# Fifteen products instead of sixteen, forked partial sums and one timed plan in a fused convolution and SwiGLU kernel

## The chip, the cores and the metric

The kernel runs on one core of one Trainium2 chip. The metric is device time of one execution in microseconds (us), lower is better. A time quoted here is the median of the fast runs of one kernel; all runs of this study were fast ones. A change of more than 2% either way counts as faster or slower, and less counts as the same.

Engines are written as in the profile: PE is TensorE's matmuls, PEld its weight loads, DVE is VectorE, ACT is ScalarE, POOL is GpSimd, SP issues transfers. "L436" is line 436 of the kernel in question. An edit that adds a line moves the numbers behind it: L586 is L587 in some experiments.

## The reference

The input is x of (8, 4096, 192) in float32. A causal convolution with 7 taps comes first (one softmaxed set of taps for each of 8 heads of 24 channels). Its 32768 tokens are normalised and go through a feed-forward block with an inner width of 1536:

```python
out = np.einsum('hk,bskhg->bshg', w, x_unf)           # 7 shifted copies of x, weighted
rms = np.sqrt(np.mean(x * x, axis=-1, keepdims=True) + 1e-06)
xn = x / rms * rms_g
g = xn @ w_gate                                        # 192 -> 1536
silu = g * (1.0 / (1.0 + np.exp(-g)))
val = xn @ w_val                                       # 192 -> 1536
return (silu * val @ w_out).astype(np.float32)         # 1536 -> 192
```

## The kernel before

The kernel works through 32 pairs of blocks of 512 tokens. For each pair there are two phases on TensorE.

In the **gate-and-value phase** four units each multiply a 3 x 3 block of weights with blocks of the normalised activations. A scheme in the manner of fast matrix multiplication needs fewer block products than plain multiplication, and pays for it with sums of weights (made once), sums of activations (`x_sums`, made for every pair on VectorE) and combinations of partial sums. Each product consists of two halves (gate in the lower rows of the array, value in the upper). The first pair uses plain products while the weight sums are made.

In the **output phase** 384 matmuls of 192 columns multiply the activated values with `w_out`. Beside it the other engines prepare later inputs: convolution, norm and transposes (`front`) for the pair after the next, and the sums of activations for the next pair.

```python
def mm(i, bk, x, first=False):                         # one product, both halves (L436)
    for h in range(2):
        rows = HALF[h]
        rhs = x[rows]
        nc.tensor.matmul(
            out=bank(h, bk)[:], lhsT=wf[u][rows, at[i], :], rhs=rhs,
            start=first, stop=True, skip_group_check=True,
        )
# ... 16 calls of mm in a unit, with copies (keep), results (res), silu and mul between them

def evac(dst, bk, n):                                  # a finished output group leaves its bank
    nc.scalar.copy(out=dst, in_=bank(0, bk)[:, 0:n])
    nc.vector.tensor_tensor(out=dst, in0=bank(1, bk)[:, 0:n], in1=dst, op=ALU.add)

# ... convolution: ScalarE multiplies each head's slice, VectorE adds a tap's product
    m = y if k == 0 else prods.tile([P, NJ, D], F32, name="m")
    for h in range(H):
        hs = slice(h * GS, (h + 1) * GS)
        nc.scalar.mul(m[:, :, hs], xk[:, :, hs], taps[:, h, k : k + 1])
    if k > 0:
        nc.vector.tensor_tensor(out=y[:], in0=y[:], in1=m[:], op=ALU.add)

# ... the driver: which step of the side work is emitted beside which group of matmuls
for p in range(PAIRS):
    # ... four units, the transposes of nxt are stepped inside them
    nxt = front(p + 2)
    sums = x_sums(p + 1)
    # ... outer(p, hts, aside): aside steps nxt and, late in the phase, sums
```

## Time and profile before

| what | value |
|---|---|
| time, median of 3 runs | 2837.64 us (2837.35 to 2837.96) |
| span of the profiled run | 2835.1 us |
| gate-and-value phase, 31 times | 54.93 us |
| output phase, 32 times | 31.33 us |
| time before the first output phase | 124.7 us |

The page's first part gives each engine's busy time, its share of the span and its count of instructions:

```profile
PE 2776.3 (98%) x20512; PEld 2206.5 (78%) x20512; DVE 2090.6 (74%) x3178; ACT 1975.9 (70%) x4753; POOL 465.3 (16%) x409
```

Two stretches of the kernel before are one output phase and the gate-and-value phase after it. The columns of this view are the window, the busy time of PE, PEld, DVE, ACT and POOL with instruction counts, the granted TensorE clock (1.00 is full), the DMA share and GB/s (the first window begins 0.27 us into its phase of 31.33 us):

```profile
988.14:1019.20 31.06, 31.06 (x383) 30.90 (x381) 20.42 (x25) 25.62 (x79) 2.06 (x2) 1.00 0.40 109
1019.20:1074.14 54.94, 54.94 (x261) 38.26 (x259) 43.98 (x74) 36.34 (x71) 10.93 (x9) 1.00 0.10 23
```

The reader should see three things: PE is busy for the whole of both windows, the clock is at full speed, and VectorE and ScalarE still have several free microseconds in each. VectorE is idle for 10.6 us of the output phase, so the engine has room for more work there, if that work comes in a good order.

### The profile page before, as it was taken

Reading aid. Unit: us, or ns where it says so; the run is one execution under the profiler, and the core shown is the slowest. Engines: PE = TensorE matmul, PEld = TensorE weight load, DVE = VectorE, ACT = ScalarE, POOL = GpSimd, SP = SyncE. Lnnn points to the kernel's source line nnn. Section 1 sums busy time; section 2 is a strip of 40 time slices with the busy share of each in tenths; the row PEclk is TensorE's granted clock in tenths of the full one; section 3 lists DMA queues with packets and bytes.
Section 4 is the critical chain, followed back from the end, with each engine's and each line's share of the span. In section 5 each row is a group of like instructions: output and inputs, shape, how many; then the busy total and the mean of one; then the engine's idle time right before and its main releaser. Section 6 shows DMA issues by size and latency. Waiting matters only on the chain.

```text
span 2835.1 us, 53033 instructions
## 1 busy us (share of the span) xinstructions
PE 2776.3 (98%) x20512; PEld 2206.5 (78%) x20512; DVE 2090.6 (74%) x3178; ACT 1975.9 (70%) x4753; POOL 465.3 (16%) x409
## 2 busy tenths in 40 slices
PE   3899999999999999999999999999999999999999
PEld 1577888778887788887788877788877888877887
DVE  7677777777777877777777777777777777777754
ACT  6567777667777677776677776777776777766733
POOL 1711111111111111111111111111111111111100
PEclk9999999999999999999999999999999999999999
DMA  6211221212221212221112212112211122111110
GB/s 156 70 48 49 65 65 46 54 43 54 65 64 42 51 46 60 65 56 43 43 54 65 65 40 59 43 54 65 60 40 50 47 65 65 48 51 43 35 45 12
DMA packets 95597, 155.18 MB, mean 55 GB/s; under 512 B 6896, under 2 KB 64752, under 8 KB 91256
## 3 DMA queue, kind: packets, MB, share of 16 engines
q1 hardware_dynamic: 94272, 150.20, 20.6%
q8 instruction: 160, 2.62, 0.4%
q0 software_dynamic: 512, 1.57, 0.2%
q14 instruction: 93, 0.76, 0.1%
q10 hardware_dynamic: 560, 0.03, 0.0%
HBM read 101.44 MB, written 50.33 MB: 54 GB/s over the span
## 4 chain that ended last, share of the span: by engine, by line
PE 97%; DVE 1%; POOL 1%; DMA 0%; issue 0%; ACT 0%; SPq 0%; DVEq 0%; POOLq 0%
PE ps L436 60%; PE ps L559 35%; PE ps L540 1%; POOL wf L228 0%; DVE nt L360 0%; DVE ht L547 0%; DMA xb<-xd 0%; DMA xd<-nt 0%; DVE wf L207 0%; POOL wf L231 0%; ACT y L344 0%; POOL o_sb L141 0%; POOL wo_sb L199 0%; DVE mf_i L202 0%; POOL r L335 0%
## 5 line engine op out<-in xcount | busy, mean ns | idle before, releaser
L436 PE MATMUL ps<-xc,wf 64*128 64x512 f32 x4960 | 1365.2, 589 | 0.0
L436 PEld LDWEIGHTS ps<-xc,wf 64*128 64x128 f32 x4960 | 781.7, 187 | 330.9 <-issue 25.5
L559 PEld LDWEIGHTS ps<-wo_sb,ht 64*128 64x128 f32 x12288 | 1013.3, 187 | 8.9 <-DVE o_sb L568 4.1
L559 PE MATMUL ps<-wo_sb,ht 64*128 64x192 f32 x12288 | 1018.1, 323 | 0.0
L436 PE MATMUL ps<-xb,wf 64*128 64x512 f32 x2976 | 939.5, 589 | 0.0
L444 ACT COPY tp<-ps 128x512 f32<-128x512 f32 x1240 | 659.9, 588 | 300.4 <-PE ps L436 300.4
L456 ACT ACTIVATE sg<-sg 128x512 f32<-128x512 f32 x744 | 475.6, 639 | 289.3 <-DVE sg L453 289.3
L436 PEld LDWEIGHTS ps<-xb,wf 64*128 64x128 f32 x2976 | 488.7, 187 | 190.1 <-issue 13.3
L453 DVE TENSOR_TENSOR sg<-ps,tp 128x512 f32<-128x512 f32 x620 | 422.8, 682 | 212.4 <-ACT tp L444 210.7
L308 DVE TENSOR_TENSOR y<-y,m 128x1536 f32<-128x1536 f32 x190 | 335.0, 1763 | 291.7 <-ACT m L304 291.3
L304 ACT ACTIVATE m<-x_sb,taps 128x192 f32<-128x192 f32 x1520 | 532.7, 441 | 6.8 <-DMA x_sb<-in_x_dram 6.1
L459 DVE TENSOR_TENSOR ht<-ht,sg 128x512 f32<-128x512 f32 x744 | 483.0, 680 | 0.0
L453 DVE TENSOR_TENSOR ht<-ps,tp 128x512 f32<-128x512 f32 x620 | 420.4, 678 | 0.0
L468 POOL TENSOR_TENSOR tp<-tp,sg 128x512 f32<-128x512 f32 x124 | 179.7, 1449 | 1208.9 <-ACT tp L444 1175.2
L332 POOL TENSOR_SCALAR r<-ss 128x8 f32<-128x8 f32 x32 | 10.0, 313 | 1075.8 <-ACT sq L320 1049.0
L568 DVE TENSOR_TENSOR o_sb<-ps,o_sb 128x192 f32<-128x192 f32 (+1 forms) x192 | 75.7, 420 | 116.6 <-ACT o_sb L567 116.6
L468 POOL TENSOR_TENSOR tp<-tp,ht 128x512 f32<-128x512 f32 x124 | 157.8, 1272 | 0.0
L344 ACT ACTIVATE y<-y,r 128x192 f32<-128x192 f32 x252 | 94.0, 445 | 84.5 <-POOL r L335 84.5
L453 DVE TENSOR_TENSOR sg<-tp,ps 128x512 f32<-128x512 f32 x124 | 85.3, 688 | 84.8 <-ACT tp L444 64.3
L567 ACT COPY o_sb<-ps 128x192 f32<-128x192 f32 (+1 forms) x192 | 66.9, 363 | 89.4 <-PE ps L559 89.2
L320 ACT ACTIVATE sq<-y 128x192 f32<-128x192 f32 x252 | 91.7, 364 | 50.6 <-DVE y L308 43.7
L540 PE MATMUL ps<-xb,wf 64*128 64x512 f32 x288 | 71.2, 626 | 54.5 <-DMA xb<-xd 44.4
(52 smaller groups left out, 773.1 us busy)
## 6 DMA issues: line engine op xcount, KB each, us to landing
xb<-xd SPq DMA_DIRECT2D x128, 384.0 KB, 6.3
x_sb<-in_x_dram SPq DMA_DIRECT2D x24, 1344.0 KB, 5.7
xd<-nt SPq DMA_DIRECT2D x128, 192.0 KB, 3.3
out_dram<-o_sb SPq DMA_DIRECT2D x64, 384.0 KB, 2.6
x_sb<-in_x_dram SPq DMA_DIRECT2D x8, 1176.0 KB, 9.1
ht<-in_moe_w_gate_dram SPq DMA_DIRECT2D x12, 192.0 KB, 8.5
ht<-in_moe_w_val_dram SPq DMA_DIRECT2D x12, 192.0 KB, 6.3
o_sb<-in_moe_w_out_dram POOLq DMA_DIRECT2D x8, 192.0 KB, 2.7
```

The source lines that it names most:

```text
L304: nc.scalar.mul(m[:, :, hs], xk[:, :, hs], taps[:, h, k : k + 1])
L308: nc.vector.tensor_tensor(out=y[:], in0=y[:], in1=m[:], op=ALU.add)
L320: nc.scalar.activation(out=sq[:], in_=y[:, j, :], func=AF.Square, accum_out=ss[:, j : j + 1])
L344: nc.scalar.mul(y[:, j, :], y[:, j, :], r[:, j : j + 1])
L436: nc.tensor.matmul(out=bank(h, bk)[:], lhsT=wf[u][rows, at[i], :], rhs=rhs, start=first, stop=True, skip_group_check=True,)
L444: nc.scalar.copy(out=t[:], in_=bank(h, bk)[:])
L453: nc.vector.tensor_tensor(out=dst, in0=in0, in1=in1, op=op)
L456: nc.scalar.activation(out=og[o][:], in_=og[o][:], func=AF.Silu)
L459: nc.vector.tensor_tensor(out=ov[o], in0=ov[o], in1=og[o][:], op=ALU.mult)
L468: nc.gpsimd.tensor_tensor(out=t[:], in0=sb["a", h][:], in1=o3, op=ALU.add)
L540: nc.tensor.matmul(out=bank(h, bk)[:], lhsT=wf[u][HALF[h], k * NF + f, :], rhs=xb[HALF[h], g, k, :], start=(k == 0), stop=(k == KP - 1), s ...
L559: nc.tensor.matmul(out=bank(h, bk)[:, w : w + D], lhsT=hts[f // NF][HALF[h], g, f % NF, j * P : (j + 1) * P], rhs=wo_sb[HALF[h], f, :], st ...
```

## The change

The intent is to take one product in sixteen out of the phase that TensorE bounds. It has five parts:

1. **15 products for 16**, with 11 sums of activations instead of 8.
2. **Forks**: a partial sum that two results need is copied from bank to bank, and both go on accumulating. The output phase writes at most 384 of a bank's 512 columns, and a new "filler" matmul of 128 columns writes the rest. No run leaves the filler out, so what happens without it is not shown.
3. **One timed plan**: a list with a time for each step of a unit, in hundredths of a product; a unit takes 1509 of them. The upper half lags 135 behind the lower one. Everything, the output phase too, goes through one heap ordered by time.
4. **Other engines**: five of six SwiGLU multiplies of a unit move to GpSimd. The first two taps of the convolution are made by VectorE alone.
5. **Transposes in the output phase**: the whole of `front` is now spread over it.

```diff
-    NW = 16
+    NW = 15
+    XOP = (5, 6, 9, 0, 15, 14, 4, 7, 13, 10, 2, 11, 12, 8, 3)
+    XSUM = (
+        (0, 1, 4), (1, 2, 6), (2, 0, 6), (9, 3, 5), (3, 3, 8), (4, 7, 15), (5, 4, 15), (6, 5, 7),
+        (7, 0, 1), (8, 1, 2), (9, 8, 15),
+    )
+    SPAN, PLAN = 1509, (
+        (0, 0, "T", "P", 4, 11, ()), (100, 0, "T", "P", 1, 4, ()), (135, 1, "T", "P", 4, 11, ()),
+        # ... cut: time, half, engine, action, operands, what it frees
+        (1840, 0, "A", "G", 3, ()), (1959, 1, "G", "M", 3, ("g3",)),
+    )
...
+    STEP = 100 * D / T
+    OUT = 2 * (T // P) * FC * STEP
+    OVER = 120
...
+        def evac(dst, bks, w):
+            put(base + n * STEP + OVER, functools.partial(low, dst, bks, w))
+            put(base + n * STEP + LAG + OVER, functools.partial(upp, dst, bks, w))
...
-        nxt = front(p + 2)
-        sums = x_sums(p + 1)
-        # ... cut: the steps beside each group
+        spread(x_sums(p + 1), base + 1650, 160, len(XSUM))
+        spread(front(p + 2, 2), base + 30, 60, 60)
+        emit(base + OUT)
```

The heap fixes the order of each engine's instructions. `spread(it, start, gap, n)` puts n steps of a generator at equal distances. The plan's times are only an order: an instruction that comes late holds up what waits for it (in the trace below PE stands still for 2.07 us, for an eviction that VectorE reaches after an addition of 1.75 us).

## The prediction

> **What bounds the kernel now.** I read the chain of work that ended last first, because a share of busy time does not say which engine sets the end.

> ```profile
> PE 97%; DVE 1%; POOL 1%; DMA 0%; issue 0%; ACT 0%; SPq 0%; DVEq 0%; POOLq 0%
> ```

> That is the page's share of the chain by engine. Its pieces in order of time (start, length, what) are:

> ```profile
> 846.66 54.94 PE ps L436 x256
> 901.60 31.33 PE ps L559 x382
> 932.93 54.94 PE ps L436 x256
> 987.87 31.33 PE ps L559 x382
> 1019.20 54.94 PE ps L436 x256
> ```

> The kernel alternates between a gate-and-value phase (L436, four units of 16 products) and an output phase (L559). PE does both without a gap, in a period of 54.94 + 31.33 = 86.27 us, 31 times. A product (two halves, two passes each) costs 54.94 / 64 = 0.858 us. So a removed product pays in full, if the other engines let PE run on.

> Second, what a step of the other engines costs, and when the chain that prepares later inputs runs. These are ScalarE, then VectorE and GpSimd, from the timeline around the same output phase:

> ```profile
> 989.70 2.86 ACT L304 ACTIVATE y<-x_sb,taps 128x192 f32<-128x192 f32 x8
> 992.47 9.08 ACT L304 ACTIVATE m<-x_sb,taps 128x192 f32<-128x192 f32 x26
> ...
> 1003.57 7.71 ACT L304 ACTIVATE m<-x_sb,taps 128x192 f32<-128x192 f32 x22
> ...
> 1013.10 0.36 ACT L320 ACTIVATE sq<-y 128x192 f32<-128x192 f32 x1 [1.33 <-DVE y L308]
> ...
> 1019.41 0.80 ACT L344 ACTIVATE y<-y,r 128x192 f32<-128x192 f32 x2 [2.44 <-POOL r L335]
> ...
> 1020.47 2.18 ACT L344 ACTIVATE y<-y,r 128x192 f32<-128x192 f32 x6
> ```

> ```profile
> 1011.31 1.76 DVE L308 TENSOR_TENSOR y<-y,m 128x1536 f32<-128x1536 f32 x1 [1.00 <-ACT m L304]
> ...
> 1013.45 1.89 DVE L393 TENSOR_TENSOR xc<-xb 128x512 f32<-128x512 f32 x3
> ...
> 1017.79 0.69 DVE L393 TENSOR_TENSOR xc<-xc 128x512 f32<-128x512 f32 x1
> ```

> The convolution fills ScalarE from 989.4 to 1011.8 (26 steps in 9.08 us: 0.345 us from start to start), then squares (0.49 us each), GpSimd's power (2.3 us), eight scalings that end at 1022.65. That is 34.8 us after the output phase began and 3.4 us after it ended: the transposes come later still, in the gate-and-value phase, where VectorE has room. The eight sums that the next products read end at 1018.48, 0.7 us before they are needed. This order is what the change alters.

> [...]GpSimd's add (L468, first half) took 1.52 us in the 90 cases where it met a VectorE multiply of two SBUF tiles, 1.27 us in the 34 others.
> [...]

> **The change part by part.**

> *Products.* 15 for 16, but the plan gives a unit 1509 hundredths of a product: 4 x 0.91 x 0.858 = 3.12 us less per pair, 31 pairs: -96.9 us (at 15.00 it would be -106).

> *Filler.* One product of 128 columns per output phase: 128/512 x 0.858 = 0.21 us, x 32 = +6.9 us.

> *The units' other engines.* In a unit of 1509 slots (12.95 us) VectorE has 19 steps of about 0.60 us (three sums took 1.89): 11.4 us. ScalarE has 14 copies of about 0.48 and six Silus of 0.53: 9.9 us. GpSimd has 7 steps of 1.27 to 1.45: 8.9 to 10.2 us. None exceeds 12.95. The tightest loop is product at slot 900, fork on ScalarE, product at 1105: 205 slots, 1.76 us. A product's second pass starts 0.43 us after its first, takes 0.59, ScalarE starts 0.04 later, a copy takes 0.59: 1.65 us and a hand-off. It fits, barely.[...] I expect units close to the plan.

> *The output phase.* Here ScalarE loses 16 of 56 convolution steps (-5.5 us); VectorE gains 8 scalings (0.23), 8 multiply-adds (0.33), loses one add of 1.76, and gains 3 sums (0.60) and 6 transposes (0.48). VectorE's total is some 28 of 31.5 us, so the sum fits. The order does not. In the built program VectorE's queue reads: the additions of the convolution, sums 1 to 5, three transposes, a sum, two transposes, a sum, a transpose, four sums. A transpose needs all eight scalings, and the second product of the next unit reads xc[9], which the eleventh sum writes. So PE now waits for the whole convolution chain. From the start of the output phase, at best:
> - two Silus end at 1.4; 40 convolution steps (13.8), one more Silu (0.5), one eviction (0.3): 16.1
> - last addition 1.8: 17.9
> - 8 squares 3.9 and two evictions 0.5: 22.3
> - GpSimd 2.4: 24.7; 8 scalings 2.8: 27.5
> - 6 transposes 2.9, 6 sums 3.6, an eviction 0.5: 34.5

> PE would want that product at 31.33 + 0.21 + 0.86 = 32.4. That is at least 2.1 us of waiting in each of 30 output phases (the last two prepare nothing).

> It may be worse. At the start of the phase three multiplies of the last unit, which the change gives to GpSimd, fall among VectorE's scalings and multiply-adds[...]: up to 3 x 1.27 us of VectorE time. About 1.4 us of delay is free; beyond it the first addition frees a product buffer too late and ScalarE waits at the fourth group. That adds 0 to 2.5 us. I choose 1.5: 3.6 us per phase, x 30 = +108 us. Bank waits inside the phase (the fifth output group needs the bank that an eviction behind the last addition frees, at about 18 to 20 us instead of 16.7) hide under this later wait.

> Sum: 2837.6 - 96.9 + 6.9 + 108 = 2855.6, say 2856 us.

> **The rivals.**
> (a) *PE stays the bound, the gain arrives*: 2837.6 - 96.9 + 6.9 = 2748 us. For it: PE was never made to wait before, and all sums of engine time fit. Against it: the order above, whose durations are those of the same instructions in this trace.
> (b) *The wait is at its floor*, with GpSimd harmless: 2748 + 30 x 2.1 = 2811 us.[...]
> (c) *The units miss the plan too*, through the 1.76 us loop or VectorE at 88%: each hundredth of a product per unit is 1.06 us, so a unit of 15.3 adds 22 us: about 2878 us[...].

> **Range and chances.** The floor of the wait is arithmetic on measured durations, so I give (a) little: it needs an error in my reading of the queue. 2% faster is below 2781 us, a wait under 1.1 us per phase: 0.07. 2% slower is above 2894, a wait of 4.9 us, or 4 with slow units: 0.17. The rest 0.76. The range runs from just below (b) to about (c): 2808 to 2900 us.

> **What would show it.** The chain: a gate-and-value phase of about 51.8 us instead of 54.94, and an output phase with its wait of 34 to 36 us, with sums and transposes on VectorE, scalings on ScalarE and GpSimd's power in the chain where before PE was 97%. Among the waits, PE waiting for a VectorE xc sum about 30 times, 2 to 5 us each. ScalarE's scalings ending about 27.5 to 30 us after the phase begins, and VectorE idle for some us before its first transpose. VectorE's multiply-adds longer than 0.41 us where a GpSimd multiply runs. The prediction is wrong if PE waits under 1 us at the start of the first unit (then my order or chain is wrong), if the units themselves take over 13.2 us each, or if PE loses its time inside the output phase at the banks and not at its end.

## The result

| kernel | median us | range | runs |
|---|---|---|---|
| before | 2837.73 | 2837.35 to 2837.96 | 4 |
| after | 2886.26 | 2885.67 to 2886.68 | 4 |

The ratio is 1.0171 (95% interval 1.0153 to 1.0189): 1.7% slower, which counts as the same. Here and below a ratio is the mean time of one kernel's fast runs over that of the other's of the same rounds, so it is not quite the ratio of the quoted medians.

The prediction of 2856 us and +18 us fell short: the measured difference is +48.5 us. The time is inside the range of 2808 to 2900 us, in part by luck: no term of the prediction had the clock in it, which turns out below to cost some 39 us.

### The profile after

The busy times, and the shares of the last chain by engine, from the page of the changed kernel:

```profile
PE 2761.5 (96%) x20144; PEld 2074.2 (72%) x20144; DVE 2433.6 (84%) x3845; ACT 2088.3 (72%) x4769; POOL 1231.5 (43%) x1033
...
PE 74%; DVE 14%; ACT 7%; issue 4%; POOL 0%; DMA 0%; DVEq 0%; SPq 0%; POOLq 0%
```

PE held 97% of the chain before; now it shares it with VectorE and ScalarE. PE's busy time fell by only 14.8 us although a fifteenth of the products' work is gone (the plan alone should save 96.9 us), so PE is also slower at what is left. The chain in order of time around one output phase (it begins at 1001.63 and ends at 1038.01; columns: start, length, what) shows where it leaves PE:

```profile
1011.77 1.75 DVE y L358
...
1013.55 1.89 ACT m L354 x6
...
1018.01 1.40 ACT m L354 x4
...
1019.62 0.15 DVE y L358
...
1021.29 0.36 DVE o_sb L610
...
1021.70 12.79 PE ps L586 x133
...
1039.46 48.02 PE ps L507 x219
```

The chain passes through the convolution (L354, L358) to an eviction (L610) and only then to PE. It does not pass through the transposes or the eleventh sum, as the prediction had it. The windows of the same phase, with the columns as before:

```profile
1001.63:1019.63 18.00, 17.93 (x205) 17.01 (x201) 17.69 (x27) 16.14 (x46) 4.43 (x4) 1.00 0.41 89
1019.63:1021.70 2.07, 0.01 (x2) 0.01 (x1) 2.07 (x4) 0.29 (x2) 0.00 (x0) 1.00 0.50 119
1022.40:1025.80 3.40, 3.40 (x26) 3.40 (x24) 2.25 (x6) 2.89 (x14) 0.22 (x1) 0.50 0.60 247
1025.80:1038.01 12.21, 12.21 (x155) 12.21 (x153) 7.30 (x14) 3.24 (x9) 2.07 (x2) 1.00 0.27 65
1038.01:1089.88 51.87, 51.87 (x248) 29.73 (x248) 45.65 (x73) 42.29 (x78) 30.75 (x25) 1.00 0.06 16
```

Read the second and third lines. PE stands still for 2.07 us in the middle of the phase, and shortly after that its granted clock is 0.50 for 3.4 us. That stretch holds 26 matmuls (22 of them start in it) where a full clock would give about 43 (the fourth line has 155 in 12.21 us, 12.7 per us). The last line is the gate-and-value phase: 51.87 us at full clock, with PE busy throughout, close to the plan's 4 x 15.09 x 0.858 = 51.8.

Why PE stands still is seen in VectorE's timeline (start, length, engine, line, operation, shapes, count; in brackets the idle time before and what ended it):

```profile
1002.40 2.99 DVE L339 TENSOR_SCALAR y<-x_sb,taps 128x192 f32<-128x192 f32 x8
...
1011.77 7.33 DVE L358 TENSOR_TENSOR y<-y,m 128x1536 f32<-128x1536 f32 x4
1019.02 0.69 DVE L440 TENSOR_TENSOR xc<-xb 128x512 f32<-128x512 f32 x1
1019.62 1.75 DVE L358 TENSOR_TENSOR y<-y,m 128x1536 f32<-128x1536 f32 x1
1021.29 0.35 DVE L610 TENSOR_TENSOR o_sb<-ps,o_sb 128x192 f32<-128x192 f32 x1
...
1030.90 1.58 DVE L410 STREAM_TRANSPOSE nt<-y 128x256 f32<-128x256 f32 x3 [4.73 <-ACT y L394]
...
1037.16 0.67 DVE L440 TENSOR_TENSOR xc<-xc 128x512 f32<-128x512 f32 x1
```

The eviction at 1021.29 frees the bank that the fifth output group needs. The eviction stands in VectorE's queue behind a sum and behind the last addition of the convolution (1019.62 to 1021.37), so PE stops at 1019.63 and goes on at 1021.70. The eleventh sum ends at 1037.83, and PE reaches the product that reads it no earlier than that. The waits of PE over the whole run (total us, times, longest) confirm that this is every phase's pattern:

```profile
PEld ps L586 <- DVE o_sb L610: 70.7, 30, 2.4
...
PE ps L586 <- DVE o_sb L610: 61.8, 30, 2.1
...
PEld ps L586 <- DVE ht L529: 10.8, 29, 0.4
```

The list has no wait of PE for an xc sum at all. A run has 30 such output phases (the last two prepare nothing). In 23 of them the clock dropped to half for 3.41 us after the pause (in one of these for twice as long); in 7 it did not.

### Where the time went

From the spans of the two profiled runs, in us:

| part | before | after | difference |
|---|---|---|---|
| up to the first output phase | 124.7 | 121.7 | -3.0 |
| 31 gate-and-value phases | 1702.9 | 1613.8 | -89.1 |
| 32 output phases | 1007.5 | 1148.7 | +141.2 |
| span | 2835.1 | 2884.2 | +49.1 |

By the medians an output phase with a clock drop takes 36.43 us, one without takes 34.75, and before they took 31.33. The drop therefore costs 1.68 us, half of the 3.41 us. The gate-and-value phase that follows a phase without a drop takes 52.67 instead of 51.87: there PE is early enough to wait 0.8 us for the eleventh sum. (The profile puts this wait down to a ScalarE copy; that it is the sum's is shown by e1, which moves only the sums and takes it away.)

### The profile page after: what moved, and what is told of

Its sections match the earlier page's. It is cut to its first block, busy times and chain, and to the rows that moved or that the text cites. A ratio compares the mean times of both kernels' runs of the same rounds, so it can differ in the third digit from the quotient of the medians.

```text
span 2884.2 us, 53991 instructions
## 1 busy us (share of the span) xinstructions
PE 2761.5 (96%) x20144; PEld 2074.2 (72%) x20144; DVE 2433.6 (84%) x3845; ACT 2088.3 (72%) x4769; POOL 1231.5 (43%) x1033
## 4 chain that ended last, share of the span: by engine, by line
PE 74%; DVE 14%; ACT 7%; issue 4%; POOL 0%; DMA 0%; DVEq 0%; SPq 0%; POOLq 0%
PE ps L507 53%; PE ps L586 19%; ACT m L354 6%; DVE y L344 5%; DVE y L339 3%; DVE y L358 2%; PE ps L557 1%; DVE ht L529 1%; DVE tile L529 1%; DVE tile L520 1%; ACT o_sb L606 0%; DVE o_sb L610 0%; POOL wf L300 0%; PE ps L597 0%; DMA xb<-xd 0%
## 5 line engine op out<-in xcount | busy, mean ns | idle before, releaser
L507 PE MATMUL ps<-xc,wf 64*128 64x512 f32 x4960 | 1516.1, 593 | 1.4 <-ACT tile L516 1.4
L586 PE MATMUL ps<-wo_sb,ht 64*128 64x192 f32 x12288 | 1123.9, 332 | 65.5 <-DVE o_sb L610 61.8
L536 POOL TENSOR_TENSOR ht<-ht,tile 128x512 f32<-128x512 f32 x620 | 784.9, 1281 | 673.7 <-DVE ht L529 266.3
L516 ACT ACTIVATE tile<-ps 128x512 f32<-128x512 f32 x992 | 571.1, 597 | 130.6 <-PE ps L507 117.6
L520 DVE COPY tile<-ps 128x512 f32<-128x512 f32 x744 | 499.9, 687 | 60.3 <-PE ps L507 47.2
L516 ACT ACTIVATE ps<-ps 128x512 f32<-128x512 f32 x744 | 410.3, 583 | 151.9 <-PE ps L507 133.6
L354 ACT ACTIVATE m<-x_sb,taps 128x192 f32<-128x192 f32 x1280 | 456.2, 443 | 62.3 <-DVE y L358 55.9
L524 POOL TENSOR_TENSOR tile<-tile,tile 128x512 f32<-128x512 f32 x248 | 310.4, 1274 | 440.2 <-ACT ps L516 350.3
L529 DVE TENSOR_TENSOR ht<-ps,tile 128x512 f32<-128x512 f32 x620 | 407.5, 683 | 13.3 <-PE ps L507 0.5
L529 DVE TENSOR_TENSOR tile<-ps,tile 128x512 f32<-128x512 f32 x620 | 403.1, 684 | 13.9
L533 ACT ACTIVATE tile<-tile 128x512 f32<-128x512 f32 x620 | 392.1, 633 | 1.1
L358 DVE TENSOR_TENSOR y<-y,m 128x1536 f32<-128x1536 f32 x160 | 281.9, 1762 | 12.6 <-ACT m L354 2.7
L529 DVE TENSOR_TENSOR ps<-ps,tile 128x512 f32<-128x512 f32 x248 | 172.6, 696 | 57.6 <-PE ps L507 56.8
L610 DVE TENSOR_TENSOR o_sb<-ps,o_sb 128x192 f32<-128x192 f32 (+1 forms) x192 | 79.8, 418 | 109.4 <-PE ps L586 66.7
```

The costliest lines, as they stand in the source:

```text
L507: nc.tensor.matmul(out=new(v, h, True) if first else old(v, h), lhsT=wf[u][HALF[h], WAT[i], :], rhs=x_op(XOP[i])[HALF[h]], start=first, st ...
L516: nc.scalar.activation(out=dst, in_=src, func=AF.Copy, scale=float(s))
L520: e.tensor_copy(out=dst, in_=src)
L524: e.tensor_tensor(out=grab((v, h)), in0=a, in1=b, op=plus(s))
L529: e.tensor_tensor(out=dst, in0=src, in1=t, op=plus(s))
L533: nc.scalar.activation(out=dst, in_=src, func=AF.Silu)
```

## The experiments

The working theory after this reading: two things hold PE back at once, the eviction behind the last addition (the pause, with the clock drop as its consequence) and the chain to the eleventh sum (the prediction's wait). They overlap, so removing either alone should give little, and removing both should give the gain back. The rival is the prediction's own account, in which the sum wait is the bound and the pause is hidden beneath it; a second rival blames GpSimd's multiplies for delaying VectorE. All kernels below gave correct results. The medians of the kernel before in the same rounds lay between 2837.47 and 2837.96 us. The first expectations count 22 and 8 phases with and without a clock drop; a recount of the trace gives the 23 and 7 used here.

### e1: the sums before the transposes

```diff
-        spread(x_sums(p + 1), base + 1650, 160, len(XSUM))
+        sums = x_sums(p + 1)
+        spread(sums, base + 1650, 0, 1)
+        spread(sums, base + 1720, 60, len(XSUM) - 1)
```

> Edit: the ten later sums of the output phase stand in VectorE's queue before the transposes; nothing else moves. Theory A (the prediction on record: the wait of the second product for the eleventh sum sets the end, 3.6 us in each of 30 phases): the wait goes, about 2780 us. Theory B (reading of the new trace: TensorE loses its time inside the phase, 2.1 us at a bank that is freed behind the last addition, and 1.7 us more by the half clock that follows that pause; the sums bind only in the 8 pairs where the clock did not drop, by 0.8 us): only 8 x 0.8 = 6 us less, about 2880 us.

Measured: 2878.91 us, ratio 1.0146 (1.0131 to 1.0161). That is 7.3 us less than the changed kernel. Every gate-and-value phase takes 51.88 us, so the 0.8 us wait is gone. Output phases still take 36.43 us, or 34.75 in eight of them and 32.98 in the first, with a pause of 2.04 us on average and 21 clock drops after it. The wait of PE in e1:

```profile
PE ps L586 <- DVE o_sb L610: 61.3, 30, 2.1
```

Removing the prediction's wait alone gains 0.3%: the wait was not what held most phases.

### e2: the eviction before the last addition

```diff
-    OVER = 120
+    OVER = 100
```

> Edit: the eviction constant is 100 for 120, which puts the first eviction of the phase before the last addition in VectorE's queue. Theory A (the sums set the end of the phase): no gain, about 2886 us, as the eleventh sum stays where it is. Theory B (bank wait and half clock): the 2.1 us pause shrinks to about 0.4, the clock does not drop, and then the eleventh sum, which ends 36.2 us after the phase began and 0.3 later here, becomes the limit: 0.7 us less in 22 pairs, about 2870 us, with TensorE waiting for VectorE's sums in nearly all pairs.

Measured: 2905.28 us, ratio 1.0238 (1.0223 to 1.0253), slower than the changed kernel. The output phase shrank to 33.35 us, but the gate-and-value phase grew to 54.34 us, or 56.04 us when the clock dropped in it (18 times). The waits of PE in e2:

```profile
PE ps L507 <- DVE xc L440: 62.0, 30, 2.1
...
PE ps L586 <- DVE o_sb L610: 12.5, 30, 0.8
```

The constant moves every eviction 20 hundredths of a product earlier in the plan, not only the first. The bank wait went from 61.8 to 12.5 us, and a wait for the eleventh sum of 2.07 us took its place 30 times. The expected 2870 us was missed because this wait dropped the clock too: 18 drops of 56.04 - 54.34 = 1.70 us are 31 us. PE's timeline and VectorE's of one such place in e2:

```profile
1039.23 0.65 PE L586 MATMUL ps<-wo_sb,ht 64*128 64x192 f32 x3
1041.94 1.43 PE L507 MATMUL ps<-xc,wf 64*128 64x512 f32 x4 [2.07 <-DVE xc L440]
```

```profile
1041.11 0.68 DVE L440 TENSOR_TENSOR xc<-xc 128x512 f32<-128x512 f32 x1
```

PE resumes when the sum that ended at 1041.79 is there. So the prediction's wait exists; in the changed kernel another wait has already made PE late when it gets there. That 2.07 us is so near the predicted floor of 2.1 us is chance: PE came to the product 1.9 us later here than it does in e8 below (output phases of 33.35 and 31.42 us).

### e3: both orders

e1 and e2 together.

> Edit: both of the two edits before. Theory A: about 2780 us, the same as with the sums moved alone. Theory B: each edit alone uncovers the other wait, together they give the gain: the output phase falls from 36.4 to about 33 us, 3.4 us less in 30 pairs, about 2785 us, below the kernel before (2838), with hardly any half-clock spells.

Measured: 2792.82 us, ratio 0.9843 (0.9828 to 0.9858). The gate-and-value phase takes 51.88 us and the output phase 33.09. No phase drops the clock. The bank wait:

```profile
PE ps L586 <- DVE o_sb L610: 12.3, 29, 0.8
```

| | sums late | sums early |
|---|---|---|
| eviction late | 2886.26 (after) | 2878.91 (e1) |
| eviction early | 2905.28 (e2) | 2792.82 (e3) |

By the 2% rule e3 still counts as the same as the kernel before; against the changed kernel one edit gains 7, the other loses 19, and both gain 93 us. That is the overlap of two waits, shown.

### e4: the first sum after the last addition

```diff
-        spread(x_sums(p + 1), base + 1650, 160, len(XSUM))
+        spread(x_sums(p + 1), base + 1720, 160, len(XSUM))
```

> Edit: the eleven sums start after the last addition instead of one before it, so that the addition and the eviction behind it come 0.6 us earlier and the pause of TensorE is about 1.5 us instead of 2.1; transposes still stand between sums. If a pause of 1.5 us still drops the clock: 0.6 us less per phase, about 2868 us and still some 20 spells of half clock. If it does not: about 2 us less at the phase's middle, of which the sums (ending about 35.6 us after the start) leave about 1.5, so about 2843 us and no spells.

Measured: 2879.74 us, ratio 1.0151 (1.0134 to 1.0168); pause 1.88 us (56.5 us in 30 phases), 21 clock drops after it. The pause was to shrink by the sum of 0.60 us that had stood before the addition, and shrank by 0.2. ScalarE's last group of multiplies (it ends at 1019.41 in the phase shown) holds the addition, so the sum filled time in which VectorE would have waited anyhow. This experiment missed its size and tells the two theories apart only weakly.

### e5: the transposes back in the units (on e2)

```diff
-        spread(front(p + 2, 2), base + 30, 60, 60)
+        nxt = front(p + 2, 2)
+        spread(nxt, base + 30, 60, 38)
+        for i in range(6):
+            put(base + OUT + (i // 2) * SPAN + (640, 1225)[i % 2], functools.partial(next, nxt, None))
+        put(base + OUT + 3 * SPAN + 30, functools.partial(next, nxt, None))
```

> Edit, on the kernel with the earlier eviction: the six transposes and the store behind them go back to the gate-and-value phase, two per unit in the first three units; the sums stay at their old times. If the transposes in VectorE's queue ahead of the sums were what held the second product in that kernel (2905 us), this gives what moving the sums gave: about 2793 us. If VectorE has no room in the units (19 steps of 0.60 us and two transposes of 0.48 in 12.95), the units grow: 0.2 us in each of three units in 30 pairs is 18 us, about 2810 us.

Measured: 2797.56 us, ratio 0.9857 (0.9843 to 0.9872). The gate-and-value phase takes 52.02 us and the output phase 33.05, without a clock drop. Moving the transposes out of the way is as good as moving the sums before them, less 0.14 us per phase that six more VectorE steps cost in the units. So it is the order of sums behind transposes that makes e2's wait, not the amount of VectorE work.

### e6: the last unit's multiplies on VectorE (on e3)

```diff
-            e = {"V": nc.vector, "G": nc.gpsimd}.get(eng)
+            last = act == "M" and u == NU - 1 and v in (2, 3, 5)
+            e = {"V": nc.vector, "G": nc.vector if last else nc.gpsimd}.get(eng)
```

> Edit, on the kernel with both orders: the three multiplies of the last unit that run after its end go from GpSimd to VectorE (0.60 us each). If GpSimd's multiplies lock VectorE out of its scalings and multiply-adds (the trace after shows 1.39 us for 0.31 once and 1.42 for 0.40 twice, 3.1 us in a phase), VectorE loses 1.8 us and gains 3.1: the last addition comes 1.3 us earlier, the pause of 0.4 us at the bank goes: 0.4 to 0.6 us less per phase, about 2778 us. If there is no lock, VectorE is 1.8 us later, the pause is about 2.2 us with the half clock behind it: above 2870 us.

Measured: 2754.58 us, ratio 0.9707 (0.9692 to 0.9721), 38 us less than e3. The output phase takes 31.78 us instead of 33.09, 1.31 us less, where I had expected 0.4 to 0.6. The pause shrank from 0.40 to 0.09 us; the other 1.0 us is PE's own way to the bank, which it reaches 17.06 us after the phase began instead of 18.06. VectorE's timeline in e6, to be read against that of the changed kernel:

```profile
1043.11 1.92 DVE L339 TENSOR_SCALAR y<-x_sb,taps 128x192 f32<-128x192 f32 x8
...
1051.18 7.33 DVE L358 TENSOR_TENSOR y<-y,m 128x1536 f32<-128x1536 f32 x4
```

The same eight scalings take 1.92 us instead of 2.99, and the first addition starts 8.07 us after them instead of 9.37, although VectorE now does three multiplies more. In the changed kernel a scaling (L339) took 0.31 us on average where no GpSimd instruction overlapped it and 0.80 where one did; a multiply-add (L344) 0.41 and 1.04. The rival with GpSimd is thus right about part of the time: 1.3 us per phase here.

### e7, e10 and e11: a pause of chosen length (on e3)

One sum stands before the last addition and the evictions in e3; here it is two, three or four.

```diff
-        spread(sums, base + 1650, 0, 1)
-        spread(sums, base + 1720, 60, len(XSUM) - 1)
+        spread(sums, base + 1650, 0, 2)                 # e7; 3 in e10, 4 in e11
+        spread(sums, base + 1720, 60, len(XSUM) - 2)    # e7; 3 in e10, 4 in e11
```

> Edit, on the kernel with both orders: two sums for one stand before the eviction, so TensorE's pause at the bank grows from 0.4 to about 1.0 us and nothing else changes. If the half clock needs a longer pause than that: 0.6 us per phase, about 2811 us, no spells. If a pause of 1.0 us drops the clock as 1.9 us did (in 22 of 30 phases, 1.7 us each): about 2848 us, some 20 spells.

Measured: 2814.03 us, ratio 0.9916 (0.9901 to 0.9931); pause 1.12 us, output phase 33.81 us, no clock drop.

> Edit, on the kernel with both orders: three sums for one before the eviction, so the pause at the bank is about 1.7 us; 0.4 and 1.1 us gave no half-clock spell in 30 phases, 1.9 and 2.1 us one in 22 or 23. If 1.7 us is still short of what drops the clock: 1.3 us per phase, about 2832 us, no spells. If it is enough: some 20 spells of 1.7 us more, about 2866 us.

Measured: 2858.59 us, ratio 1.0073 (1.0058 to 1.0088); pause 1.72 us, output phase 34.41 without and 36.09 with a clock drop, of which there were 16. The waits of PE in e10:

```profile
PE ps L586 <- DVE o_sb L610: 51.5, 30, 1.7
```

From e7 to e10 the pause grew by 0.6 us x 30 = 18 us and the time by 44.6; the remaining 26.6 are 16 drops of 1.68 us. The cost of a pause jumps once the clock joins in.

What decides whether it does? In the nine traces counted below, all changes of the granted clock within a trace lie at whole multiples of 3.413 us from each other. I laid that grid over the traces that I had by then and asked how much of one slice PE had stood still. With the grid moved by 0.27 us (the shift and the half below are both fitted to these traces), no pause with less than half a slice (1.71 us) in any single slice was followed by a drop, and nearly all others were. This was found afterwards, so two more kernels tested it.

> Four sums now stand between the last addition and the evictions instead of three, so TensorE's pause grows by one sum of 0.60 us from 1.72 to about 2.32 us. A rule found in the traces of the runs so far, and not predicted before them: the granted clock changes only at whole multiples of 3.413 us, and it halves for one such slice when TensorE was idle for at least half of one slice (1.71 us), with the slices taken 0.27 us later than the record of the clock has them. It holds in 201 of 212 pauses, none of them below half a slice dropping. It expects here: every pause with under 1.71 us in one slice keeps the clock, nearly every other drops it, some 20 to 30 of 30 phases. Time: 2858.6 + 30 x 0.6 + 4 to 14 more drops x 1.7, so 2883 to 2901 us. If instead only the length of the pause mattered and two microseconds were sure to drop it, all 30 would drop, those with under half a slice too.

Measured: 2893.49 us, ratio 1.0195 (1.0178 to 1.0212), which is inside the range; whether it is over 2% slower than the kernel before is unclear. The pause is 2.33 us (1.68 in the first phase). By the rule, 26 of the 30 pauses had half a slice or more in one slice: all 26 dropped the clock. Three others, equally long but split between two slices (at most 0.46 of a slice in one), kept it, and so did the first. The rival in which only length matters is out.

### e12: a pause of 1.4 us (on e6)

The edit of e10, on e6.

> The kernel with the three multiplies on VectorE and three sums before the evictions: the pause should be about 1.4 us (1.72 us less the 0.3 us that those multiplies took off the pause before). The rule of half a slice (1.71 us) expects not one of 30 phases to drop the clock, an output phase of about 31.42 + 1.4 + 1 = 33.8 us and a time of 2754.6 + 30 x 2.0 to 2.3 = 2815 to 2824 us. If the risk of a drop only grows with the length of the pause (none at 1.1 us, 16 of 30 at 1.72 us), about half way between should give some 8 drops, and 14 us more: 2829 to 2838 us.

Measured: 2795.43 us, ratio 0.985 (0.9835 to 0.9865). The pause was 1.42 us (in two phases 1.77) and no phase dropped the clock, as the rule has it and against the 8 drops of the rival. The two of 1.77 us, 0.52 of a slice, are exceptions just above the line. The time fell below my range of 2815 to 2824: I had added 1 us per phase that I took to go with any pause. The output phase took 33.11 us, which is e8's 31.42, the pause and 0.27. So that microsecond goes with GpSimd's multiplies, and not with the pause.

The count over nine kernels with pauses (half a slice is taken as 0.495 and over; after, e1, e2, e4, e7, e9, e10, e11, e12):

| largest part of the pause in one slice | pauses | followed by a drop |
|---|---|---|
| under half a slice | 125 | 0 |
| half a slice or more | 147 | 134 |

Of the 13 exceptions, 7 lie between 0.499 and 0.519 of a slice; 6 are e2's, where the pause lies among the wide products, and they stay unexplained. Each of the 134 drops fills the slice right after the one with the larger part of the pause.

### e9: the multiplies on VectorE in the changed kernel

The edit of e6 alone, applied to the changed kernel.

> Edit, on the changed kernel itself: only the three late multiplies of the last unit go from GpSimd to VectorE; eviction and sums keep their places. The last addition and all behind it come 1.3 us earlier. Then TensorE's pause at the bank is about 0.8 us, without a half clock, and the eleventh sum ends about 34.9 us after the phase began instead of 36.2 and becomes the limit in every pair, as the prediction had it: 2.3 us less in 22 pairs and 1.4 in 8, about 2824 us (the prediction's rival with GpSimd harmless said 2811). If the wait for the sum, about 1.5 us, drops the clock, up to 35 us more, about 2858 us.

Measured: 2835.81 us in 12 runs, ratio 0.9992 (0.9984 to 1.0001), so 50 us less than the changed kernel and as fast as the kernel before. The eleventh sum ended 34.93 us after the phase began (36.2 in the changed kernel), as expected. The pause shrank only from 2.06 to 1.75 us, where 0.8 was expected, since the eviction came 1.3 us earlier but PE also reached it 1.0 us earlier. The waits of PE in e9:

```profile
PEld ps L587 <- DVE o_sb L611: 61.4, 30, 2.1
...
PE ps L587 <- DVE o_sb L611: 52.6, 30, 1.8
```

A pause of 1.75 us is just over half a slice, and only 9 phases dropped the clock instead of 23: 14 x 1.68 = 23.5 of the 50 us. PE's earlier arrival is worth 30 x 1.0 = 30 us and the shorter pause 30 x 0.3 = 9 us; the wait for the eleventh sum, which now binds in 21 phases instead of 7 (gate-and-value phase 52.67 us), takes 14 x 0.8 = 11 us back.

### e8: all together (on e6)

```diff
-        spread(sums, base + 1650, 0, 1)
-        spread(sums, base + 1720, 60, len(XSUM) - 1)
+        spread(sums, base + 1720, 55, len(XSUM))
```

> Edit, on the kernel with the last multiplies on VectorE: all sums after the last addition, so the eviction is another 0.6 us earlier. If the pause is already gone with the multiplies moved: the same 2778 us. If something of it is left: down to about 2770 us. Not below 2760: the units' 51.88 us and an output phase of at least 31.5 us, 31 times, with 138 us of start and last phase, give 2748 us, and the crossings between the phases cost some 0.3 to 0.8 us more each.

Measured: 2741.08 us, ratio 0.9658 (0.9642 to 0.9674): 3.4% faster than the kernel before and, by the medians, 5.0% faster than the changed one (2741.08 / 2886.26 = 0.950). It is faster than the 2760 us that I had given as the least: the crossings between the phases, for which I had added time, cost nothing. The gate-and-value phase takes 51.81 us, the plan's length, and the output phase 31.42. Its chain is PE alone again:

```profile
1373.07 26.74 PE ps L587 x327
1399.81 0.02 PE ps L598
1399.83 1.23 PE ps L587 x14
...
1404.74 50.74 PE ps L508 x235
```

Compare the output phase with the changed kernel's chain: the 26.74 us run without a break over the place where PE had stood still. This version keeps every part of the change but the last three multiplies of a pair on GpSimd, and gets the whole of the intended gain (96.9 us by the plan) by order and by moving these three multiplies.

## Why the prediction was wrong in size

**Products, -96.9 us: right.** The gate-and-value phase fell to 51.87 us, so 31 x (51.87 - 54.93) = -94.9. The measured sum is -89.1, because the eleventh sum is waited for in 7 phases of 52.67 (7 x 0.8 = 5.6). The tight loop of 1.76 us in the units held, VectorE at 88% held, and GpSimd did no harm there (51.87 us against the plan's 51.8). Rival (c), which puts the loss in the units, landed nearest in time and was wrong in mechanism.

**Filler, +6.9 us: too large.** In e8, where nothing else is in the way, the whole output phase is 0.09 us longer than before, 2.9 us in 32 phases.

**The chain to the eleventh sum, +108 us: right in its steps.** The scalings ended 29.2 us after the phase began (predicted 29.0 with the delay of 1.5), the transposes waited 4.73 us for them, and the eleventh sum ended at 36.2 (predicted 36.0). What GpSimd's multiplies cost VectorE was about what the sum's 1.5 us stood for (e6 took 1.3 us of it away). One reading is off, and nothing rests on it: the convolution fills ScalarE from 989.70 to 1011.28, not from 989.4 to 1011.8.

**"Bank waits inside the phase [...] hide under this later wait": this step failed.** The bank wait itself was foreseen ("at about 18 to 20 us instead of 16.7"): the bank came free 20.0 us after the phase began, and PE had wanted it at 18.0. In the 7 phases without a clock drop even the conclusion holds: output and gate-and-value phase together take 34.75 + 52.67 = 87.42 us against e8's 31.42 + 51.81 = 83.23, a loss of 4.19 us set by the eleventh sum. The prediction's own sum for the two is 31.33 + 0.21 + 3.6 + 51.81 = 86.95 us. But in 23 phases PE came to the eleventh sum after it was ready. The pause had halved the clock for 3.41 us, which cost 1.68 us more, and those phases lose 36.43 + 51.87 - 83.23 = 5.07 us. A wait can only hide under a later one if PE, after the wait, runs as fast as it would have. That was the assumption, and it was not written down.

The terms for the wait and the filler were thus mis-sized by two amounts: in 23 pairs the clock drop costs 0.88 us more than the sum wait that it displaces, 20 us; and a pair without a drop is 87.42 - 86.95 = 0.47 us longer than predicted, 14 us in 30 pairs. With -3 us for the start, this gives the missing 30 us.

What fills the 138 us that the output phases lost beyond the filler: the pause 61.8, the clock 23 x 1.68 = 38.6, and a rest of about 38 us. Some 30 us of the rest come before the pause and with GpSimd's multiplies: PE reaches the bank 18.06 us after the phase began, and 17.06 us in e9, which moves only those multiplies. In this stretch two waits of the weight loads are seen in the trace, for `ht` (10.8 us) and for ScalarE's eviction (9.9 us), and both are gone in e9 and e12. The other 0.27 us per phase stay in e9 and e12 beside the pause; I have not assigned them, and they are gone in e8.

The prediction's own list of what would make it wrong ended with "if PE loses its time inside the output phase at the banks and not at its end". That is what happened.

**The clock.** The prediction had no term for it. In these traces the slices are 3.413 us long, and pauses of 1.72 to 2.33 us often halved the clock for one of them.

**GpSimd and VectorE.** The prediction's 1.5 us, out of at most 3 x 1.27 us, was an estimate: of the two engines' meeting, it had from the trace before only that GpSimd's add took 1.52 us where it met a VectorE multiply and 1.27 us elsewhere. The runs show the other side: scalings took 0.80 us instead of 0.31 beside GpSimd, multiply-adds 1.04 instead of 0.41, and moving three multiplies per pair away gained 38 us (e6) and 50 us (e9; 23.5 of these are clock drops avoided).

## What to carry to other kernels

When a change fills an engine's queue, list where each instruction stands that frees something for the bound engine, and place it ahead of long instructions that it doesn't depend on (here an addition of 1.75 us; with the eviction ahead of it, the bank wait went from 61.8 to 12.5 us in e2). Two waits that overlap hide each other: removing one may show nothing or a loss (here one edit alone gained 7 us, the other lost 19, and both gained 93), so test them together before dropping either. In these runs a pause of TensorE of 1.72 us or more often cost another 1.68 us in clock, so a wait "hidden" under a later one should be counted with that.
